# A polynomial-sketch attention and gated feed-forward kernel on one Trainium2 core: batch 1's values loaded ahead of batch 2's queries, other planned durations, and a new set of due times

## The chip, the cores and the metric

The kernel runs on one core of one Trainium2 chip. The metric is the device time of one execution in microseconds. Three runs of the kernel before gave 99.48, 100.64 and 100.89 us, a median of 100.64. A fourth execution, the one that was profiled, took 99.95 us, of which 98.2 lie between the first and the last instruction (the span); every duration below comes from that one.

The engines are called PE (TensorE), DVE (VectorE), ACT (ScalarE), POOL (GpSimd) and SP (SyncE, which here issues nearly all DMAs).

## What is computed

Attention with a product of two small sketches in place of a softmax, then a gated feed-forward block, in these steps (batch 4, heads 4, sequence 1088, head size 32, sketch size 8):

```python
def phi(x):                       # 32 numbers -> 8 x 8 products
    a = einsum('rd,bhsd->bhsr', S1, x); b = einsum('rd,bhsd->bhsr', S2, x)
    return (a outer b).reshape(..., 64)
q_p, k_p = phi(q), phi(k)
kv  = einsum('bhsf,bhsd->bhfd', k_p, v);  z = k_p.sum(axis=2)
x   = einsum('bhsf,bhfd->bhsd', q_p, kv) / (einsum('bhsf,bhf->bhs', q_p, z) + 1e-06)
x   = x.transpose(0, 2, 1, 3).reshape(4352, 128)
out = (maximum(x @ w_gate, 0) * (x @ w_val)) @ w_out      # 128 -> 1536 -> 128
```

## The kernel before

**Tiling.** The feed-forward half is cut into 103 units, numbered 0 to 102. A unit is one bank of the accumulator memory: up to 512 columns of tokens times feed-forward blocks. Unit u is made of these instructions: `g u` (PE, gate product, line 966), `relu u` (ACT, line 971), `v u` (PE, value product, line 978), `h u` (DVE, gate times value, line 988) and `o u` (PE, output product, line 1000). In every sixth unit from 4 on the product goes over POOL: `vcp u` (ACT, line 983) copies the value out of the accumulator, and `hp u` (POOL, line 993) multiplies. A group's last unit ends with `oe u` (ACT, line 1008) and the store `st u` (SP, lines 1017 to 1020). The first six units hold the first 256 tokens; they use the weights third by third, so units 4 and 5 need the last third.

**What stands before it, batch by batch.** For batch b: `kt1 b` (DVE, transposes the keys, line 532), `ksk b` (PE, both sketches of the keys, line 543), `kt2 b` (DVE, transposes them back, line 556), `z b` and `w b` (PE, lines 571 and 585, the sum for the denominator) with the small DVE steps `zc b` and `wc b`, `kphi b` (the outer product, line 600, on POOL; for batch 0 the last two of five pieces are on DVE, by way of an extra transpose into the accumulator, `kt2b`, line 564), `vc b` (casts v to 16 bits, line 607), `kv b` (PE, line 614) and `kve b` (DVE, line 621). On the query side: `qt1 b` (DVE, line 1040), `qsk` (PE, line 736), `qt2` (DVE, line 742), `bw`, `dn`, `rd` and `an` (lines 770, 777, 782 and 802, the denominator and the division), `qphi` (the outer product, line 868, on POOL after the first set). Then a transpose: for the first three groups on PE (`qtr`, line 886) and ACT (`qpt`, line 893), for the other seven a transposing DMA (`qtd`, line 876, issued by SP). `num` (PE, line 902) and `x` (line 909 or 914) give the tokens that the gate and value products read. Batch 0 is split: its first 256 tokens are one set (`0,0`), the rest another (`0,2`).

**Weights.** They arrive as 32-bit thirds (gate `wg0` to `wg2`, value `wv0` to `wv2`, output `wo0` to `wo2`) and are parked in buffers that later hold keys, queries and values: `wst`, lines 251 to 253. A cast (lines 427 and 429, on ACT or POOL by the table `CAST`, line 420) makes 16-bit weights of each and frees its buffer. So a late load waits for a cast: batch 1's v for the cast of the third that was parked in it, batch 2's keys for two others (lines 445 to 451). Batch 2's queries (`q2`) wait for no cast.

**What sets the order.** A planner (class `Plan`, lines 36 to 144) places every step on its engine by the durations that the code gives, by when buffers and accumulator banks come free, and by a due time. Due times follow from the unit numbers (lines 926 and 386 to 387; `D1` is added from unit 6 on) and from a table of hand-made offsets, `shift` (line 1113). Loads are in the plan as instants (`LAND`, line 406) or durations (line 443). The plan's order on each engine is what is built; while the kernel runs, only semaphores decide, and each engine works through its own queue in order. Until the first unit, PE is kept at work by filler matmuls on zeros (line 331).

Of the kernel before, what the change touches and what calls it, by code (L numbers as in the profile page):

```python
# [147 lines left out]
def kernel(  # L148
# [12 lines left out]
    nc = tc.nc  # L161

    B, H, S, D = q.shape
# [46 lines left out]
    def load_k(eng, b):  # L210
        eng.dma_start(out=k_sb[b][:, 0:NC * D], in_=flat(k, b))
# [34 lines left out]
    def half(t, i):  # L246
        return t[:, i * W3:(i + 1) * W3]
# [2 lines left out]
    v1, v2 = (v32[b].rearrange("p h c -> p (h c)") for b in (1, 2))  # L250
    wst = [[half(k_sb[3], 0), half(q_sb[3], 0), half(v2, 0)],
           [half(k_sb[3], 1), half(q_sb[3], 1), half(v2, 1)],
           [half(k_sb[2], 0), half(k_sb[2], 1), half(v1, 0)]]

    def load_w(i):
        c = slice(i * W3, (i + 1) * W3)
# [16 lines left out]
    def load_q(eng, b):  # L273
        eng.dma_start(out=q_sb[b], in_=flat(q, b))

    def load_vs(b):
        for a in (0, 2, 1, 3):
            load_v(nc.sync, b, a)
# [105 lines left out]
    P.banks[S_BANK] = 6.0  # L384
    l_sx = Lease()
    T0, U, SLACK = 11.0, 0.65, 0.25
    D1 = 0.2

    TURN = ["ACT"] * 3 + ["DMA"] * 7

# [12 lines left out]
    def pool(cols):  # L403
        return cols * 0.00188 + 0.07

    LAND = {"k0a": 3.6, "S": 4.3, "k0b": 4.25, "q0a": 5.4, "q0b": 7.3, "v0": 9.75, "wg0": 10.1,
            "wv0": 10.74, "wg1": 11.38, "wv1": 12.02, "wo0": 12.66, "wg2": 13.3, "wv2": 14.94,
            "wo1": 15.58, "k1": 16.94, "wo2": 17.58, "q1": 18.94}
    land = {n: P.landed(n, t) for n, t in LAND.items()}
    P.free["DMA"] = LAND["q1"]  # L410

    def bank(l, i=0):
# [5 lines left out]
    wb_op = P.add("DVE", "WB", 0.15, make_WB, [land["S"]], rec=0.07)  # L418

    CAST = {"wg0": "ACT", "wv0": "POOL", "wg1": "ACT", "wv1": "ACT", "wo0": "POOL",  # L420
            "wg2": "ACT", "wv2": "POOL", "wo1": "POOL", "wo2": "POOL"}
    wcast = {}

    def cast(w, i, eng):
# [12 lines left out]
    issue = {}  # L437

    def load(name, fn, after):
        n = 4 if name[0] == "v" else 1  # L440
        issue[name] = i = P.add("SP", f"{name} issue", 0.44 * n, fn, after,
                                rec=1.95 - 0.44 * n)
        land[name] = P.add("DMA", name, 2.7 if n == 4 else 1.4, None, [i], rec=0.15)

    load("v1", lambda: load_vs(1), [wcast["wo2"]])
    load("k2", lambda: load_k(nc.sync, 2), [wcast["wo0"], wcast["wo1"], issue["v1"]])
    load("q2", lambda: load_q(nc.sync, 2), [])
    load("v2", lambda: load_vs(2), [wcast["wg2"], wcast["wv2"], land["v1"]])
    load("k3", lambda: load_k(nc.sync, 3), [wcast["wg0"], wcast["wv0"]])
    load("q3", lambda: load_q(nc.sync, 3), [wcast["wg1"], wcast["wv1"]])  # L450
# [2 lines left out]
    class K:  # L453


        def __init__(self, b, prev):
# [11 lines left out]
                        rec=0.07)  # L468
# [21 lines left out]
            self.wc_op = P.add("DVE", f"wc {b}", 0.11, self.wc, [w], drop=[lw], rec=0.07)  # L490
            phis = []
            cut = [(0, 2), (2, 4), (4, 6), (6, KX)] if b else [(0, 2), (2, 4), (4, 6), (6, 8), (8, KX)]
            own = [3, 4] if b == 0 else []
            lb = Lease()
            self.lb = lb
            for n, (lo, hi) in enumerate(cut):
# [11 lines left out]
                else:  # L508
                    phis.append(P.add("POOL", f"kphi {b} {lo}", pool(cols),
                                      lambda lo=lo, hi=hi: self.phi(nc.gpsimd, lo, hi), dep))  # L510
            vc = [P.add(e, f"vc {b} {h}", 0.66 if e == "POOL" else 0.58,
                        lambda h=h, e=e: self.vc(h, e), [land[f"v{b}"]],
                        rec=0.0 if e == "POOL" else 0.13)
                  for h, e in enumerate(["ACT", "ACT" if b else "POOL"])]
            lm = Lease()
            self.lm = lm
            self.kvs = []
# [84 lines left out]
                in0=src[:, 0, :, :, None].to_broadcast([128, n, R, R]),  # L602
                in1=bs[:, :, None, :].to_broadcast([128, n, R, R]), op=ALU.mult)

        def vc(self, h, e):
            o, i = (t[self.b][:, 2 * h:2 * h + 2] for t in (v16, v32))
            nc.scalar.copy(out=o, in_=i) if e == "ACT" else nc.gpsimd.tensor_copy(out=o, in_=i)  # L607

        def kv(self, lo, hi, pp):
            m = bank(self.lm)  # L610
# [196 lines left out]
    class G:  # L807


        def __init__(self, qs, b, ks, x0, n, i, col, old, how):  # L810
            self.qs, self.x0, self.n, self.col = qs, x0, n, col
            self.ks, self.b = ks, b
            i = i % NQ
            self.qp, self.pt = q_qp[i], q_pt[i]
            name = f"{self.b},{qs.x0 + x0}"
            phis = []
            if qs.first:
                for x in range(n):
                    phis.append(P.add("DVE", f"qphi {name} {x}", 0.31,
                                      lambda x=x: self.phi(nc.vector, x, x + 1), [qs.o4],  # L820
                                      drop=[qs.la], rec=0.07))
                qs.la.left -= n
            else:
                phis.append(P.add("POOL", f"qphi {name}", pool(n * 256) - 0.02 * n,
                                  lambda: self.phi(nc.gpsimd, 0, n), [qs.o4] + old))
            if how == "DMA":
                pt = P.add("SP", f"qtd {name}", 1.28, self.xpose, phis + old, rec=0.7)
                self.turn = pt
                pt = P.add("DMA", f"qtd {name}", 0.6, None, [pt], rec=0.5)
            else:  # L830
                lt = Lease()
                self.lt = lt
                trs = []
                for x in range(n) if qs.first else [None]:
                    lo, hi = (x, x + 1) if x is not None else (0, n)
                    trs.append(P.add("PE", f"qtr {name} {lo}", pe16(2 * (hi - lo), 128),
                                     lambda lo=lo, hi=hi: self.tr(lo, hi),
                                     [phis[lo] if qs.first else phis[0]], take=[lt]))
                pt = P.add(how, f"qpt {name}",
                           n * 256 / 1920.0 + 0.085 if how == "DVE" else act(n * 256),  # L840
                           lambda: self.tre(how), trs + old, drop=[lt],
                           rec=0.07 if how == "DVE" else 0.13)
            self.pt_op = pt
            ln = Lease()
            self.ln = ln
            num = P.add("PE", f"num {name}", pe16(2, n * 128) if b is not None else
                        pe16(8, 64), self.num,
                        [pt] + [kk.kve for kk in self.ks], take=[ln])
            if qs.first:
                self.x_op = P.add("DVE", f"x {name}", dve(n * 128), self.x_div, [num, qs.rdc],  # L850
                                  drop=[ln], rec=0.07)
            else:
                self.x_op = P.add("ACT", f"x {name}", act(n * 128), self.x, [num], drop=[ln],
                                  rec=0.13)
            self.last = [num, pt] + phis
            qs.last += phis
# [185 lines left out]
    qt1 = {}  # L1042
# [64 lines left out]
    for o in P.ops:  # L1107
# [3 lines left out]


    shift = {
# [24 lines left out]
    }  # L1138
    for o in P.ops:
        o.due += shift.get(o.name, 0.0)  # L1140
# [46 lines left out]
```

## Time and profile before

| what | value |
|---|---|
| median of three runs (lowest, highest) | 100.64 us (99.48, 100.89) |
| the profiled execution: time, span | 99.95 us, 98.2 us |
| granted TensorE clock, mean | 0.995 |
| first gate product (`g 2`) begins | 14.08 us |
| last output products end, last eviction begins | 95.07, 95.09 us |
| idle time of the PE array from 14 us to the end of its work | 0.4 us |
| busy from 25 to 40 us, out of 15: PE, DVE, ACT, POOL | 15.00, 14.80, 14.20, 13.78 us |
| batch 1's v: four issues by SP from 19.05 us | land 2.7 to 3.0 us after the issue |
| batch 2's queries: issued at 12.52 us | land 7.6 us after the issue |

A line of the timeline reads: start, length, engine, source line, operation, output and inputs with their shapes, how many in a row, and in square brackets the idle time before it and what ended it. In the view by windows each engine's entry is its busy time in that stretch and, in brackets, its instructions.

### The profile page before, as it was taken

Reading aid. Unit: us, or ns where it says so; the run is one execution under the profiler, and the core shown is the slowest. Engines: PE = TensorE matmul, PEld = TensorE weight load, DVE = VectorE, ACT = ScalarE, POOL = GpSimd, SP = SyncE. Lnnn points to the kernel's source line nnn. Section 1 sums busy time; section 2 is a strip of 40 time slices with the busy share of each in tenths; the row PEclk is TensorE's granted clock in tenths of the full one; section 3 lists DMA queues with packets and bytes.
Section 4 is the critical chain, followed back from the end, with each engine's and each line's share of the span. In section 5 each row is a group of like instructions: output and inputs, shape, how many; then the busy total and the mean of one; then the engine's idle time right before and its main releaser. Section 6 shows DMA issues by size and latency. Waiting matters only on the chain.

```text
span 98.2 us, 3002 instructions
## 1 busy us (share of the span) xinstructions
PE 93.0 (95%) x1130; PEld 62.1 (63%) x1130; DVE 83.3 (85%) x181; ACT 81.4 (83%) x160; POOL 61.1 (62%) x66
## 2 busy tenths in 40 slices
PE   5979999999999999999999999999999999999960
PEld 2247667866685665665646765777577756768850
DVE  5969987989999999999999899948869676789850
ACT  3402799987999988999998759999999999999930
POOL 6129639789979799699859924999540404314000
PEclk9999999999999999999999999999999999999998
DMA  2999999559830668960436002104480220030031
GB/s 50 308 278 263 405 411 414 218 136 273 259 111 0 147 131 282 321 176 5 108 83 140 0 7 77 30 23 94 107 157 10 53 60 0 0 80 27 0 107 53
DMA packets 16782, 13.26 MB, mean 135 GB/s; under 512 B 8064, under 2 KB 14464, under 8 KB 16768
## 3 DMA queue, kind: packets, MB, share of 16 engines
q1 hardware_dynamic: 16592, 12.95, 45.1%
q8 instruction: 8, 0.13, 0.6%
q10 hardware_dynamic: 176, 0.13, 0.4%
q14 instruction: 6, 0.05, 0.2%
HBM read 9.14 MB, written 2.23 MB: 116 GB/s over the span
## 4 chain that ended last, share of the span: by engine, by line
PE 87%; DMA 5%; DVE 3%; SPq 1%; issue 0%; ACT 0%; DVEq 0%
PE ps L1000 24%; PE ps L966 23%; PE ps L978 22%; DMA q_sb<-in_q_dram 5%; PE ps L902 4%; PE ps L736 3%; PE ps L331 2%; PE ps L614 2%; PE ps L543 2%; PE ps L886 1%; PE ps L571 1%; DVE kab L556 1%; PE ps L585 1%; DVE ht L988 1%; DVE kp L600 1%; PE ps L755 1%
## 5 line engine op out<-in xcount | busy, mean ns | idle before, releaser
L988 DVE TENSOR_TENSOR ht<-g_sb,ps 128x512 f16<-128x512 f16 (+1 forms) x87 | 55.2, 672 | 8.3 <-PE ps L978 4.3
L971 ACT ACTIVATE g_sb<-ps 128x512 f16<-128x512 f32 (+1 forms) x103 | 56.6, 607 | 4.0 <-PE ps L966 2.7
L966 PE MATMUL ps<-xT,wg 128*128 128x512 f16 (+1 forms) x120 | 35.7, 349 | 0.0
L978 PE MATMUL ps<-xT,wv 128*128 128x512 f16 (+1 forms) x120 | 34.8, 347 | 0.0
L1000 PEld LDWEIGHTS <-ht 128*128 128x128 f16 x408 | 25.9, 98 | 9.3 <-DVE ht L988 2.4
L1000 PE MATMUL ps<-wo,ht 128*128 128x128 f16 x408 | 30.7, 219 | 0.4 <-DVE ht L988 0.4
L993 POOL TENSOR_TENSOR ht<-g_sb,v_sb 128x512 f16<-128x512 f16 x16 | 18.7, 1167 | 17.0 <-ACT v_sb L983 9.2
L600 POOL TENSOR_TENSOR kp<-kab 128x512 f16<-128x512 f32 (+1 forms) x15 | 17.0, 1162 | 2.5 <-DVE kab L556 2.3
L966 PEld LDWEIGHTS <-wg 128*128 128x128 f16 x120 | 12.8, 115 | 6.5 <-issue 1.8
L978 PEld LDWEIGHTS <-wv 128*128 128x128 f16 x120 | 13.0, 114 | 5.1
L868 POOL TENSOR_TENSOR qqp<-qan,qabc 128x1024 f16<-128x1024 f32 (+1 forms) x9 | 15.7, 1755 | 0.7 <-DVE qan L802 0.6
L983 ACT COPY v_sb<-ps 128x512 f32<-128x512 f32 x16 | 9.7, 608 | 0.3 <-PE ps L978 0.2
L331 PE MATMUL ps<-zero 128*128 128x512 f16 (+5 forms) x24 | 7.1, 430 | 1.0 <-DVE maskkv L296 1.0
L1040 DVE STREAM_TRANSPOSE qT<-q_sb 128x576 f32<-128x576 f32 (+4 forms) x10 | 6.0, 611 | 0.9 <-DMA q_sb<-in_q_dram 0.9
L1008 ACT ACTIVATE o_sb<-ps 128x512 f32<-128x512 f32 (+1 forms) x10 | 5.4, 539 | 1.6 <-PE ps L1000 1.5
L607 ACT CAST v<-v 128x576 f16<-128x576 f32 x7 | 4.6, 684 | 1.5 <-DMA v<-in_v_dram 1.5
L532 DVE STREAM_TRANSPOSE kT<-k_sb 128x544 f32<-128x544 f32 (+2 forms) x8 | 5.5, 720 | 0.0
L742 DVE STREAM_TRANSPOSE qabc<-ps 128x512 f32<-128x512 f32 (+2 forms) x8 | 5.4, 698 | 0.1
L902 PE MATMUL ps<-qpt,bz 128*128 128x512 f16 (+2 forms) x26 | 5.3, 306 | 0.0
L914 ACT CAST xT<-ps 128x512 f16<-128x512 f32 (+1 forms) x9 | 5.0, 561 | 0.3 <-PE ps L902 0.3
L331 PEld LDWEIGHTS <-zero 128*128 128x128 f16 x24 | 2.4, 116 | 3.3 <-issue 1.4
L770 POOL TENSOR_TENSOR bw<-qabc 128x256 f32<-128x256 f32 (+1 forms) x3 | 2.3, 773 | 2.8 <-DVE qabc L742 2.8
(85 smaller groups left out, 64.0 us busy)
## 6 DMA issues: line engine op xcount, KB each, us to landing
v<-in_v_dram SPq DMA_DIRECT2D x15, 144.0 KB, 5.6
out_dram<-o_sb SPq DMA_DIRECT2D x28, 64.0 KB, 1.8
k_sb<-in_k_dram SPq DMA_DIRECT2D x3, 544.0 KB, 4.0
q_sb<-in_q_dram SPq DMA_DIRECT2D x3, 544.0 KB, 7.3
k_sb<-in_moe_w_out_dram SPq DMA_DIRECT2D x2, 256.0 KB, 5.0
q_sb<-in_q_dram SPq DMA_DIRECT2D x1, 416.0 KB, 5.7
k_sb<-in_k_dram SPq DMA_DIRECT2D x1, 288.0 KB, 2.9
k_sb<-in_k_dram SPq DMA_DIRECT2D x1, 256.0 KB, 3.0
```

The lines of the kernel that those rows point to most:

```text
L331: nc.tensor.matmul(PS[:, W_BANK, 0:m * w], zero, zero[:, None, 0:w].to_broadcast([128, m, w]), start=True, stop=True)
L600: eng.tensor_tensor(out=self.kp[:, lo:hi].rearrange("p x g (i a c) -> p (x g i) a c", i=2, a=R), in0=src[:, 0, :, :, None].to_broadcast([1 ...
L868: eng.tensor_tensor(out=self.qp[:, lo:hi].rearrange("p x g (i a c) -> p (x g i) a c", i=2, a=R), in0=a_in[:, :, :, None].to_broadcast([128 ...
L902: nc.tensor.matmul(o[:, 0:n * 128].rearrange("f (x t) -> f x t", x=n)[:, :, t], self.ks[b or 0].bz[:, p], self.pt[:, 0:n, p, t], start=(p ...
L966: nc.tensor.matmul(bank(self.lg)[:, y * W:(y + 1) * W], wblock(wg, j), x, start=True, stop=True, skip_group_check=True)
L971: nc.scalar.activation(out=self.gs[:, 0:self.cols], in_=bank(self.lg)[:, 0:self.cols], func=ACTF.Relu)
L978: nc.tensor.matmul(bank(self.lv)[:, y * W:(y + 1) * W], wblock(wv, j), x, start=True, stop=True, skip_group_check=True)
L983: nc.scalar.copy(out=self.vs, in_=bank(self.lv))
L988: nc.vector.tensor_tensor(out=self.ht[:, 0:w], in0=self.gs[:, 0:w], in1=bank(self.lv)[:, 0:w], op=ALU.mult)
L993: nc.gpsimd.tensor_tensor(out=self.ht, in0=self.gs, in1=self.vs, op=ALU.mult)
L1000: nc.tensor.matmul(o[:, s], self.ht[:, y * W + s * 128:y * W + (s + 1) * 128], wo[:, j // 4, (j % 4) * DM:(j % 4 + 1) * DM], start=(j == 0 ...
L1040: nc.vector.transpose(qT[b][:, lo * 32:hi * 32], q_sb[b][:, lo * 32:hi * 32])
```

## The change

It moves which third is parked where, gives some steps to other engines, alters numbers in the plan and replaces the table of offsets. Counted in instructions, DVE loses three (the extra transpose and two outer products of batch 0's keys), POOL gains two outer products and the cast of `wg2` and loses the cast of half of batch 0's v, and ACT gains that cast and loses `wg2`'s. All other work is the same and stands in another order.

```diff
-           [half(k_sb[2], 0), half(k_sb[2], 1), half(v1, 0)]]
+           [half(k_sb[2], 0), half(v1, 0), half(k_sb[2], 1)]]
...
-    D1 = 0.2
+    D1 = 0.7
...
-    LAND = {"k0a": 3.6, "S": 4.3, "k0b": 4.25, "q0a": 5.4, "q0b": 7.3, "v0": 9.75, "wg0": 10.1,
-            "wv0": 10.74, "wg1": 11.38, "wv1": 12.02, "wo0": 12.66, "wg2": 13.3, "wv2": 14.94,
-            "wo1": 15.58, "k1": 16.94, "wo2": 17.58, "q1": 18.94}
+    LAND = {"k0a": 3.6, "S": 4.3, "k0b": 4.25, "q0a": 5.4, "q0b": 7.5, "v0": 10.0, "wg0": 10.35,
+            "wv0": 10.99, "wg1": 11.63, "wv1": 12.27, "wo0": 12.91, "wg2": 13.55, "wv2": 15.09,
+            "wo1": 15.73, "k1": 17.09, "wo2": 17.73, "q1": 19.09}
...
-            "wg2": "ACT", "wv2": "POOL", "wo1": "POOL", "wo2": "POOL"}
+            "wg2": "POOL", "wv2": "POOL", "wo1": "POOL", "wo2": "POOL"}
...
-        land[name] = P.add("DMA", name, 2.7 if n == 4 else 1.4, None, [i], rec=0.15)
-
-    load("v1", lambda: load_vs(1), [wcast["wo2"]])
-    load("k2", lambda: load_k(nc.sync, 2), [wcast["wo0"], wcast["wo1"], issue["v1"]])
-    load("q2", lambda: load_q(nc.sync, 2), [])
+        land[name] = P.add("DMA", name, {"k2": 3.6}.get(name, 2.7 if n == 4 else 1.4), None, [i], rec=0.15)
+
+    load("v1", lambda: load_vs(1), [wcast["wo1"]])
+    load("q2", lambda: load_q(nc.sync, 2), [issue["v1"]])
+    load("k2", lambda: load_k(nc.sync, 2), [wcast["wo0"], wcast["wo2"], issue["q2"]])
...
-            own = [3, 4] if b == 0 else []
+            own = [] if b == 0 else []
...
-                  for h, e in enumerate(["ACT", "ACT" if b else "POOL"])]
+            vc = [P.add("ACT", f"vc {b} {h}", 0.58, lambda h=h: self.vc(h), [land[f"v{b}"]],
+                        rec=0.13) for h in range(2)]
...
-                pt = P.add("DMA", f"qtd {name}", 0.6, None, [pt], rec=0.5)
+                pt = P.add("DMA", f"qtd {name}", 2.4 if b == 3 else 0.6, None, [pt], rec=0.5)
...
-        "g 10": -0.4, "g 12": -2.5, "g 16": 0.9, "g 18": 0.4, "g 19": 1.3, "g 2": -3.4,
+        "an 0,2": -3.3, "bw 0,0": -0.9, "bw 2,0": -0.9, "dn 0,0": -3.2, "g 11": -3.1,
...
```

The order that follows, where the prediction speaks of it (everything built, in the order of each engine's queue):

| queue | before | after |
|---|---|---|
| PE, first units | `num 0,0, g 2, v 0, g 0, v 2, g 1, v 1, qtr 0,2, g 3, g 4, g 5, v 3, o 0, num 0,2, o 1, qtr 0,4, v 4` | `num 0,0, g 0, v 0, g 1, qtr 0,2, v 1, g 2, g 4, v 2, g 3, num 0,2, g 5, v 3, o 0, o 1, qtr 0,4, o 2, g 8, v 4` |
| PE, before the keys | `ksk 0, sx, qaT, z 0` | `ksk 0, qaT, sx, z 0` |
| DVE, set 0,2 | `qt2, qt2, qt1, bw, kve 0, dn, rd, x 0,0, an` | `qt2, qt2, qt1, bw, dn, rd, an, kve 0, x 0,0` |
| ACT, first stage | `vc 0, rdx, wg0, qpt, rdTe, wg1, wv1, wg2, relu` | `rdx, vc 0, vc 0, qpt, rdTe, wg0, wv1, wg1, relu` |
| ACT, batch 1's v | `oe 5, relu 12, relu 10, relu 9, vcp 10, vc 1, relu 11, relu 13, vc 1` | `oe 5, relu 7, vc 1, vc 1, relu 9, vcp 10` |
| POOL | `kphi 0` x3, `vc 0, wv0, wo0, qphi 0,2, qphi 0,4, wv2, wo1, wo2, hp 4` | `kphi 0` x5, `wv0, qphi 0,2, wo0, wg2, qphi 0,4, wo1, wv2, wo2, hp 4` |
| SP | `q2, v1, k2, st 5` | `v1, q2, k2, st 5` |
| SP, batch 3 | `qtd 3,0, st 59, qtd 3,4` | `qtd 3,0, qtd 3,4, st 59` |

More of the change, by code (lines that the diff above doesn't have):

```diff
@@ L510, in __init__ @@
                                       lambda lo=lo, hi=hi: self.phi(nc.gpsimd, lo, hi), dep))
-            vc = [P.add(e, f"vc {b} {h}", 0.66 if e == "POOL" else 0.58,
-                        lambda h=h, e=e: self.vc(h, e), [land[f"v{b}"]],
-                        rec=0.0 if e == "POOL" else 0.13)
-                  for h, e in enumerate(["ACT", "ACT" if b else "POOL"])]
+            vc = [P.add("ACT", f"vc {b} {h}", 0.58, lambda h=h: self.vc(h), [land[f"v{b}"]],
+                        rec=0.13) for h in range(2)]
             lm = Lease()
@@ L603, in phi, with vc @@
                 in1=bs[:, :, None, :].to_broadcast([128, n, R, R]), op=ALU.mult)
-        def vc(self, h, e):
-            o, i = (t[self.b][:, 2 * h:2 * h + 2] for t in (v16, v32))
-            nc.scalar.copy(out=o, in_=i) if e == "ACT" else nc.gpsimd.tensor_copy(out=o, in_=i)
+        def vc(self, h):
+            nc.scalar.copy(out=v16[self.b][:, 2 * h:2 * h + 2], in_=v32[self.b][:, 2 * h:2 * h + 2])
         def kv(self, lo, hi, pp):
```

51 rows, old and new, of the table shift are left out of this document.

## The prediction

> **What bounds the kernel now.** I read the page first: engine totals, the chain that ended last, the granted clock.
>
> ```profile
> PE 93.0 (95%) x1130; PEld 62.1 (63%) x1130; DVE 83.3 (85%) x181; ACT 81.4 (83%) x160; POOL 61.1 (62%) x66
> ...
> PEclk9999999999999999999999999999999999999998
> ...
> PE 87%; DMA 5%; DVE 3%; SPq 1%; issue 0%; ACT 0%; DVEq 0%
> ```
>
> 87% of the chain is PE, at full clock. Whether PE is at its pace is seen in the chain in order of time (start, length, line, how many) and in PE's waits from 14 us to the end:
>
> ```profile
> 40.47 1.08 PE ps L978 x5
> ...
> 43.32 0.89 PE ps L1000 x16
> ```
>
> ```profile
> PE ps L1000 <- DVE ht L988: 0.4, 1, 0.4
> ```
>
> Five 512-column matmuls take 1.08 us, 0.217 each; four 128-column ones take 0.223. A unit costs PE 0.217 + 0.217 + 0.223 = 0.66 us. In 81 us the array waited once, 0.4 us, near the end (last `h` to last `o`). So from the first gate product PE is the bound, and a step made earlier anywhere else, after 14 us, is worth nothing unless PE waits for it. What a change can win is the time before the first unit, plus the 0.4. What it can lose is open-ended: each new PE wait is added in full. Last I looked at how much the others have left, 25 to 40 us (busy time of PE, PEld, DVE, ACT, POOL):
>
> ```profile
> 25.00:40.00 15.00, 15.00 (x202) 9.68 (x201) 14.80 (x28) 14.20 (x28) 13.78 (x12) 1.00 0.58 162
> ```
>
> DVE idles 0.2 us in 15. That is the thin cover.
>
> **The first stage.** Here the order changes most. The rows of DVE and POOL before:
>
> ```profile
> 12.50 0.34 DVE L770 TENSOR_TENSOR bw<-qabc 128x192 f32<-128x192 f32 x1
> 12.76 0.28 DVE L621 TENSOR_TENSOR bz<-ps,maskkv 128x128 f16<-128x128 f32 x1
> 12.96 0.37 DVE L777 TENSOR_REDUCE qdn<-bw 128x24 f32<-128x216 f32 x1
> 13.37 0.30 DVE L782 RECIPROCAL qrd<-qdn 128x24 f32<-128x24 f32 x1
> 13.60 0.42 DVE L909 TENSOR_TENSOR xT<-ps,rdT 128x256 f16<-128x256 f32 x1
> 13.95 0.35 DVE L802 TENSOR_TENSOR qan<-qabc,qrd 128x192 f32<-128x192 f32 x1
> ```
>
> ```profile
> 11.32 0.62 POOL L429 CAST wv<-k_sb 128x512 f16<-128x512 f32 x1 [0.27 <-DMA k_sb<-in_moe_w_val_dram]
> 13.18 0.61 POOL L429 CAST wo<-k_sb 128x512 f16<-128x512 f32 x1 [1.25 <-DMA k_sb<-in_moe_w_out_dram]
> 14.37 2.98 POOL L868 TENSOR_TENSOR qqp<-qan,qabc 128x512 f16<-128x512 f32 x2 [0.58 <-DVE qan L802]
> 17.30 0.61 POOL L429 CAST wv<-v 128x512 f16<-128x512 f32 x1
> ...
> 19.78 1.17 POOL L993 TENSOR_TENSOR ht<-g_sb,v_sb 128x512 f16<-128x512 f16 x1 [0.76 <-ACT v_sb L983]
> ```
>
> In the before column, `v 4` begins at 17.96, right after the cast of `wv2` (17.30 + 0.61). So POOL's queue, not the first gate product at 14.08, sets when the units run freely.
>
> *DVE, after.* It loses the extra transpose (0.36) and two outer products (0.69, 0.41). `z 0` now stands behind `qaT` and `sx`, so its end moves from 7.90 to about 8.17. From there in steps of before's starts: `zc` 8.18, two transposes of the queries to 9.23, `bw 0,0` 9.29, its five followers 1.25 to 10.54, two `qt2` 0.97, the small transpose 0.13: `bw 0,2` at 11.64 instead of 12.50. Then `dn` 12.01, `rd` 12.41, `an` 12.76 to 13.10. But `kve 0` now stands behind `an`: it starts at 13.03 instead of 12.76, though its matmuls end by 12.4 (POOL's fifth outer product ends near 11.7, `vc 0`'s second half near 11.9). From `kve` to the first gate product the step was 14.08 - 12.76 = 1.32: the first unit starts at 14.35, 0.27 later.
>
> *POOL, after.* Five `kphi 0`: four steps of 1.03 from 7.00 reach 11.11; the fifth is 128x256, and 768 columns take 1.52, 512 take 1.07, so 0.6: 11.7. `wv0` to 12.25; wait for `an`, 13.13; `qphi 0,2` to 14.16; `wo0`, `wg2` (0.56 each) to 15.28; `qphi 0,4` 1.90 to 17.18; `wo1` 17.73; `wv2` ends 18.35, 0.44 later than before. Between first unit and `v 4`, PE has two more products than before in front of it (`o 2`, `g 8`), 0.22 + 0.22 = 0.44 us of work that no longer follows. Run from 14.35, PE reaches `v 4` at about 18.3 and waits to 18.4. `g 4` comes at 15.7, after `wg2` at 15.3. **First stage: 0.0 us.** The 0.27 is lost in time that PE would have waited anyway; 1.5 us more on POOL is hidden in its old gaps (1.25, 0.58, 0.27) and in the earlier `an`. ACT gains one cast of 0.67, loses one of 0.62: nothing, covered by `rdT`, which is ready at 12.7.
>
> **Unit 4.** On ACT `qpt 0,4` (1.09) and `vcp 4` (0.69) now stand behind `x 0,2` and `relu 5`: `x 0,2` ends near 18.1, `relu 5` starts 17.9, `qpt` 18.4, `vcp` ends 20.0, `hp 4` (1.17) 21.2. PE reaches `o 4` at 20.9. **+0.3 us**; bounds 0 (if ACT is as early as before, 19.70) and 0.5.
>
> **Loads.** `v1` waits for the cast of `wo1` (17.8) instead of `wo2` (19.03): issued 1.2 us earlier. Four issues took 2.5 us and landed 2.7 to 3.0 after issue, with one 544 KB load finishing 1.1 us after the first issue; after, the load of `q1` stands in the same relation (18.83). So v lands near 22.6. `q2` no longer goes at 12.52 but behind v, at 20.3, and `k2` behind that, after the cast of `wo2` (18.9), at 20.8 instead of 21.62; `st 5` behind them needs its eviction at 22.6, so SP holds nothing up. Needed: `kv 1` stands at 27.3 in both orders by the sum of PE's work (0.217, 0.223, and the rows of the small products), `ksk 2` at 30.7 (before 32.2), queries of batch 2 later still. Between ends of 3 us (v1) and 7.6 (q2, then in a crowd) all land by 28. **0.0 us**, and nothing gained, because nothing waited for v1. The longer durations for `k2` and `qtd 3,0` move work away from transfers that were not late: `qtd 3,0` is issued at 64.8 and lands 2.7 later; `num 3,0` runs at 70.8.
>
> **The long middle.** The same PE steps in another order: from `v 4` to the end the sum of rows is 76.1 us before, 75.6 after (18.4 to 94.0; the two products again). What matters is whether DVE keeps up. The tightest run after is `v 8` to `o 21`: 13 products at 0.605, two `qt2` 0.65, two `kt1` 0.67, `qt1` 0.69 and 0.62, `kt2` 0.71, `kve` 0.21, `dn` 0.47, `rd` 0.30 = 13.50 us, 0.25 for the first `v` to get out, against 13.82 of PE work: 0.07 us to spare. The same sum over before has its least at `o 18`, 0.14, and no wait is seen there. **0.0 us**; bounds -0.1 and +0.5, some 0.01 on each of 22 steps and a second such run (`o 38`, 0.30 to spare).
>
> **The end.** After the last full group's `o`, five products remain on DVE in both orders, so the 0.4 us stays; bounds -0.4 and 0.
>
> **Sum:** 0 + 0.3 + 0 + 0 + 0 = +0.3 us on the profiled execution's 99.95 (span 98.2 + 1.75 around it) = 100.25. That execution lies 0.69 below the median of three; all four together average 100.24, which I take as base for another median: **100.5 us**, no change that can be told, as a measurement of this kernel resolves about 2% (98.6 to 102.7).
>
> **A rule that speaks against it.** The only DVE operations with two inputs in SBUF before the units are `bw 0,2` and `an 0,2`, and before, both ran while POOL was idle (11.94 to 13.18, 13.80 to 14.37), so no row shows them beside POOL. After, `bw 0,2` at 11.64 meets POOL's cast of `wv0` (11.7 to 12.3). If one holds the other for its length, `bw` starts up to 0.6 late, and `an`, `qphi`, `wv2` and the first unit with it. The Trainium skill, SBUF — State Buffer, "Who interferes with whom", says a VectorE instruction with two SBUF inputs and a GpSimd one that reads SBUF exclude each other, whoever starts first; by that rule 0.6 us is added, 101.1.
>
> **Rivals.**
> - *Slower: ACT stands still at batch 1's v.* Before, ACT came to `vc 1` at 25.09, 1.3 us after v had landed (23.8). After, it stands behind `relu 7`, near 23.0, against a landing at 22.6: 0.4 to spare. All of ACT queues behind it: `relu 9`, `vcp 10`, and so DVE's `h 9`, on the run with 0.07 to spare. Against: the 3.0 us of this very load. For: the page's median for v is 5.6, and batch 3's took 5.9 to 6.7 behind two 544 KB loads. With 5.6 from the last issue at 20.0 v lands at 25.6, ACT is held 2.6 us; work that PE has in hand hides some 0.5 (an estimate: two products whose banks are free, 0.44): +2.1, 102.6. It decides, beyond 2%, from a landing at about 25.7 on.
> - *The two engines exclude each other*, the 0.6 above, all of it on the path through `an` and `wv2`: 100.5 + 0.6 = 101.1.
> - *Faster: POOL's chain ends earlier.* If DVE's relief comes through with `an` at 12.7, POOL's wait (12.25 to 13.13) shrinks by 0.4, `wv2` and `v 4` come 0.4 earlier, the wait at `o 4` is gone, and the last wait may go (0.4): 100.24 - 0.4 - 0.4 = 99.4. Against: `an` needs nine DVE steps whose lengths are known. PE's pace leaves no more than this.
>
> **How the numbers follow.** No change as summed, 0.56: the sum rests on rows, and PE's own work is the same to 0.1 us. Exclusion, 0.12: no row for or against it. ACT held, 0.20: one row against, an average for it; 0.04 of this is shorter holds that stay within 2%, 0.16 goes beyond. Faster, 0.12: two things have to come at once; 0.04 of it I give to more than 2%, as single runs of before spread by 1.4 us. So faster by over 2% 0.04, within 2% 0.56 + 0.12 + 0.04 + 0.08 = 0.80, slower by over 2% 0.16. The range that leaves 0.2 out runs from just under the faster case to the held one: 99.3 to 102.6. The likeliest case alone, by its bounds (0 and 0.5 at unit 4, -0.1 and +0.5 in the middle, -0.4 at the end): 99.7 to 101.2.
>
> **What would show it.** First gate product at 14.3 and `v 4` at 18.4, just behind the cast of `wv2`; POOL's wait before `qphi 0,2` shrunk; `hp 4` ending near 21.2 with PE's weight load waiting for it; ACT not idle before `vc 1`; PE without waits of over 0.3 us from 22 to 92. Wrong: an idle ACT before line 604 (the v cast), several PE waits on `ht` between 25 and 50, or a first unit at 13.7 or before.

## The result and the profile after

| | before | after |
|---|---|---|
| median (runs; lowest, highest) | 99.86 us (22; 98.95, 101.64) | 100.58 us (22; 99.88, 101.67) |
| the profiled execution: time, span | 99.95, 98.2 us | 100.27, 98.5 us |
| ratio, 95% interval | | 1.0070 [1.0048, 1.0093] |

The medians hold every run; the ratios leave out runs over 1.5% above the fastest of the same kernel.

The change costs 0.7 us. The number forecast, 100.5, lies 0.1 below the time measured, but that is luck: two errors of opposite sign made it fit. The kernel before takes 99.86 and not the 100.24 that was put under the sum, and the loss is 0.5 to 0.7 us and not 0.3. So "no change" was wrong: there is a small loss.

The page after. PE's total is 93.4 us for 93.0, and the chain that ended last has 80% of PE for 87%, because it now runs back through a transfer in the first stage:

```profile
PE 93.4 (95%) x1131; PEld 62.8 (64%) x1131; DVE 82.7 (84%) x178; ACT 81.1 (82%) x160; POOL 62.7 (64%) x68
...
PE 80%; DMA 12%; SPq 2%; DVE 1%; issue 1%; POOL 1%; ACT 0%; DVEq 0%
```

PE's waits from 13 us on (us in total, times, longest), and the stretch from 25 to 40 us (busy time of PE, PEld, DVE, ACT, POOL):

```profile
PE ps L963 <- POOL wg L429: 0.6, 1, 0.6
```

```profile
25.00:40.00 15.00, 14.97 (x200) 9.69 (x199) 14.68 (x28) 13.77 (x27) 14.29 (x12) 1.00 0.58 157
```

Before's wait of 0.4 at the end is gone from this list, and a new one of 0.6 stands in the first stage: `g 4` waits for the cast of `wg2`. The rows of DVE and POOL that answer to those shown of before:

```profile
10.68 0.34 DVE L767 TENSOR_TENSOR bw<-qabc 128x192 f32<-128x192 f32 x1
...
11.81 0.36 DVE L799 TENSOR_TENSOR qan<-qabc,qrd 128x192 f32<-128x192 f32 x1
12.09 0.28 DVE L618 TENSOR_TENSOR bz<-ps,maskkv 128x128 f16<-128x128 f32 x1
```

```profile
12.25 1.07 POOL L865 TENSOR_TENSOR qqp<-qan,qabc 128x512 f16<-128x512 f32 x1 [0.67 <-DVE qan L799]
...
14.78 0.62 POOL L429 CAST wg<-v 128x512 f16<-128x512 f32 x1 [0.91 <-DMA v<-in_moe_w_gate_dram]
15.36 1.95 POOL L865 TENSOR_TENSOR qqp<-qan,qabc 128x1024 f16<-128x1024 f32 x1
17.26 0.61 POOL L429 CAST wo<-v 128x512 f16<-128x512 f32 x1
17.81 0.62 POOL L429 CAST wv<-v 128x512 f16<-128x512 f32 x1
```

`bw 0,2` comes at 10.68 (forecast 11.64), `an` at 11.81 (12.76). But POOL gets nothing out of it: it stands idle for 0.91 us in front of `wg2`, which lands late, and ends `wv2` at 18.43, where 18.35 was forecast. On PE:

```profile
13.40 0.38 PE L963 MATMUL ps<-xT,wg 128*128 128x256 f16 x2
...
15.45 0.41 PE L963 MATMUL ps<-xT,wg 128*128 128x256 f16 x2 [0.57 <-POOL wg L429]
...
18.48 0.84 PE L975 MATMUL ps<-xT,wv 128*128 128x256 f16 x6
...
19.48 0.71 PE L541 MATMUL ps<-kT,wS 64*32 64x288 f32 x16
...
21.06 0.39 PE L997 MATMUL ps<-wo,ht 128*128 128x128 f16 x4
21.55 0.35 PE L569 MATMUL ps<-kab 128*32 128x32 f32 x18
...
25.05 0.38 PE L975 MATMUL ps<-xT,wv 128*128 128x256 f16 x2
```

The row at 19.48 is `ksk 1`. Up to it both orders have run the same number of products, so its start can be compared directly; before it was at

```profile
19.41 0.71 PE L543 MATMUL ps<-kT,wS 64*32 64x288 f32 x16
...
93.51 1.54 PE L1000 MATMUL ps<-wo,ht 128*128 128x128 f16 x24 [0.36 <-DVE ht L988]
```

Before takes 93.51 + 1.54 - 19.41 = 75.64 us from `ksk 1` to the last output product; after, the last row is

```profile
93.25 2.09 PE L997 MATMUL ps<-wo,ht 128*128 128x128 f16 x24
```

and the stretch 93.25 + 2.09 - 19.48 = 75.86 us. So in this pair 0.07 us are lost ahead of `ksk 1` and 0.22 behind it. The wait at the end has not gone: the same 24 products now wait in small pieces inside 2.09 us. The list of waits hides this, as it hides some 0.2 us each at `z 1` (0.49 from `o 4` at 21.06 to 21.55, where before takes 0.31) and at `v 9` (25.05; eight matmuls of 0.055 from 24.41 end by 24.85).

### The profile page after: what moved, and what is told of

The parts are those of the page before. It is cut to its first block, busy times and chain, and to the rows that moved or that the text cites. A ratio compares the mean times of both kernels' runs of the same rounds, so it can differ in the third digit from the quotient of the medians.

```text
span 98.5 us, 2985 instructions
## 1 busy us (share of the span) xinstructions
PE 93.4 (95%) x1131; PEld 62.8 (64%) x1131; DVE 82.7 (84%) x178; ACT 81.1 (82%) x160; POOL 62.7 (64%) x68
## 4 chain that ended last, share of the span: by engine, by line
PE 80%; DMA 12%; SPq 2%; DVE 1%; issue 1%; POOL 1%; ACT 0%; DVEq 0%
PE ps L997 23%; PE ps L975 22%; PE ps L963 22%; DMA v<-in_moe_w_gate_dram 6%; DMA v<-in_v_dram 5%; PE ps L899 4%; PE ps L733 2%; PE ps L541 2%; PE ps L611 2%; DVE ht L985 1%; PE ps L569 1%; POOL wg L429 1%; PE ps L883 1%; PE ps L583 1%; SPq L235 0%
## 5 line engine op out<-in xcount | busy, mean ns | idle before, releaser
L968 ACT ACTIVATE g_sb<-ps 128x512 f16<-128x512 f32 (+1 forms) x103 | 55.7, 612 | 4.2 <-PE ps L963 3.3
L963 PE MATMUL ps<-xT,wg 128*128 128x512 f16 (+1 forms) x120 | 34.9, 348 | 0.6 <-POOL wg L429 0.6
L975 PE MATMUL ps<-xT,wv 128*128 128x512 f16 (+1 forms) x120 | 33.8, 348 | 0.0
L997 PE MATMUL ps<-wo,ht 128*128 128x128 f16 x408 | 31.7, 219 | 0.1
L997 PEld LDWEIGHTS <-ht 128*128 128x128 f16 x408 | 26.7, 98 | 7.9 <-DVE ht L985 1.1
L598 POOL TENSOR_TENSOR kp<-kab 128x512 f16<-128x512 f32 (+2 forms) x17 | 18.6, 1125 | 1.3 <-DVE kab L554 1.3
L331 PE MATMUL ps<-zero 128*128 128x512 f16 (+4 forms) x25 | 7.1, 404 | 1.0 <-DVE maskkv L296 1.0
L1037 DVE STREAM_TRANSPOSE qT<-q_sb 128x512 f32<-128x512 f32 (+4 forms) x10 | 6.0, 604 | 0.0
L604 ACT CAST v<-v 128x576 f16<-128x576 f32 x8 | 5.2, 676 | 0.4 <-DMA v<-in_v_dram 0.3
L611 PEld LDWEIGHTS <-kp 128*128 128x128 f16 (+1 forms) x72 | 3.2, 98 | 1.5 <-issue 0.3
```

The costliest lines, as they stand in the source:

```text
L331: nc.tensor.matmul(PS[:, W_BANK, 0:m * w], zero, zero[:, None, 0:w].to_broadcast([128, m, w]), start=True, stop=True)
L598: eng.tensor_tensor(out=self.kp[:, lo:hi].rearrange("p x g (i a c) -> p (x g i) a c", i=2, a=R), in0=src[:, 0, :, :, None].to_broadcast([1 ...
L963: nc.tensor.matmul(bank(self.lg)[:, y * W:(y + 1) * W], wblock(wg, j), x, start=True, stop=True, skip_group_check=True)
L968: nc.scalar.activation(out=self.gs[:, 0:self.cols], in_=bank(self.lg)[:, 0:self.cols], func=ACTF.Relu)
L975: nc.tensor.matmul(bank(self.lv)[:, y * W:(y + 1) * W], wblock(wv, j), x, start=True, stop=True, skip_group_check=True)
L997: nc.tensor.matmul(o[:, s], self.ht[:, y * W + s * 128:y * W + (s + 1) * 128], wo[:, j // 4, (j % 4) * DM:(j % 4 + 1) * DM], start=(j == 0 ...
```

## The experiments

Each kernel is compared with the kernel before on the same chip. Times in us; `v 4`, `ksk 1` and the stretch from `ksk 1` to the end of the last output product are from the one profiled execution of each, the medians from many. A profiled execution need not be a usual one: that of e3 is the fastest of its twelve, 99.88 against a median of 100.50.

| kernel | median (runs) | ratio to before | `v 4` | `ksk 1` | `ksk 1` to last `o` |
|---|---|---|---|---|---|
| before; once more (b1) | 99.86 (22); 100.52 (1) | | 17.96; 17.85 | 19.41; 19.29 | 75.64; 75.64 |
| after | 100.58 (22) | 1.0070 [1.0048, 1.0093] | 18.48 | 19.48 | 75.86 |
| after, once more (a2) | 100.38 (12) | 1.0046 [1.0012, 1.0080] | 18.46 | 19.46 | 76.12 |
| e1 | 100.60 (12) | 1.0061 [1.0028, 1.0094] | 18.53 | 19.50 | 75.73 |
| e2 | 100.74 (12) | 1.0067 [1.0029, 1.0106] | 18.31 | 19.31 | 76.56 |
| e3 | 100.50 (12) | 1.0091 [1.0058, 1.0124] | 18.13 | 19.11 | 75.84 |
| e4 | 100.51 (12) | 1.0065 [1.0026, 1.0103] | 17.59 | 18.59 | 76.19 |
| e5 | 101.15 (6) | 1.0130 [1.0063, 1.0196] | 18.35 | 19.35 | 76.63 |
| e6 | 101.64 (6) | 1.0168 [1.0111, 1.0226] | 19.10 | 20.08 | 76.69 |
| g1 | 100.64 (12) | 1.0078 [1.0045, 1.0111] | 18.11 | 19.19 | 76.22 |
| g2 | 100.44 (12) | 1.0060 [1.0024, 1.0096] | 18.20 | 19.20 | 76.38 |
| g3 | 100.54 (12) | 1.0054 [1.0018, 1.0090] | 17.91 | 18.99 | 76.31 |
| g4 | 101.79 (6) | 1.0184 [1.0128, 1.0240] | 18.51 | 20.22 | 77.30 |
| before, delayed (d1) | 102.72 (6) | 1.0289 [1.0232, 1.0346] | 20.30 | 21.75 | 75.63 |
| after, delayed (d2) | 103.12 (6) | 1.0337 [1.0266, 1.0407] | 20.77 | 21.77 | 76.06 |

### The last gate third and the order of the loads (e1 to e4)

First theory A: the loss is the wait at `g 4` and POOL's queue behind the cast of `wg2`. Rivals: B, it is spread over the order behind unit 4; C, it is the loads' new order. The edits, in the order of each queue:

```diff
e1 -POOL wo0, wg2, qphi 0,4        -ACT relu 1, qpt 0,2
   +POOL wo0, qphi 0,4             +ACT relu 1, wg2, qpt 0,2
e2 -PE v 1, g 2, g 4, v 2, g 3, num 0,2, g 5, v 3, o 0
   +PE v 1, g 2, v 2, g 3, num 0,2, v 3, g 4, g 5, o 0
e3  both
e4 -SP v1, q2, k2
   +SP q2, v1, k2
```

> The changed kernel with one edit: the cast of the last gate third is given back to ACT, where it stands behind relu 1 (as for ACT, so for POOL all other orders stay). Theory A (the loss lies at the last gate third: PE waits 0.57 us for its cast at g 4, and POOL's qphi 0,4, wo1 and wv2 queue behind the same cast): PE's wait at g 4 stays, as the third lands at 14.7 whoever casts it, but POOL's qphi 0,4 starts near 13.9 instead of 15.36 and wv2 ends near 17.2 instead of 18.4, so v 4 comes 0.3 to 0.4 us earlier: about 100.2 against 100.6. Theory B (the first stage costs nothing, the loss is in the order after unit 4): within 0.1 of the changed kernel. Theory C (the loss comes from the loads' new order): within 0.1.

> The changed kernel with one edit: on PE, g 4 and g 5 stand behind v 3, so that products which need no late weights fill PE's 0.57 us wait. The cast of the third stays on POOL. Theory A in its POOL form (the queue behind the cast is what counts): v 4 still waits for wv2 at 18.4, so 0 to -0.1 us, about 100.5. If PE's wait at g 4 is itself the loss: -0.5, about 100.0. Theory B: within 0.1 of 100.6. Theory C: within 0.1.

> Both edits: the cast of the last gate third on ACT, and g 4 and g 5 behind v 3. Theory A: neither PE's wait nor POOL's queue is left, v 4 near 17.5 to 17.7 instead of 18.48, so -0.7 to -0.9 us: about 99.8, as fast as the kernel before or a little faster. More than the sum of the two alone if each hides the other. Theory B: less than 0.2 gained. Theory C: within 0.1.

> The changed kernel with one edit: batch 2's queries are issued ahead of batch 1's v again, without a wait, as before. Theory C (the loads' new order is what costs): -0.5 to -0.7 us, about 100.0. Theories A and B: nothing waits for either load, so within 0.15 of 100.6, with v landing up to 1 us later behind the 544 KB of queries and ACT idle before its cast by up to that.

All four take 100.50 to 100.74, as the changed kernel does. The wait moves where the cast goes: in e1 PE waits 0.6 for ACT's cast of `wg2`, in e3 0.6 at `num 0,2`, whose `qpt` stands on ACT behind that cast. In e2 the wait at `g 4` is gone and another has come. PE's wait, and ACT's rows at batch 1's v, of e2:

```profile
PE ps L975 <- ACT g_sb L968: 0.7, 1, 0.7
```

```profile
23.79 1.25 ACT L604 CAST v<-v 128x576 f16<-128x576 f32 x2 [0.80 <-DMA q_sb<-in_q_dram]
24.95 0.59 ACT L968 ACTIVATE g_sb<-ps 128x512 f16<-128x512 f32 x1
```

ACT reaches the cast 0.80 before v has landed (the row names the transfer of `q2`, which runs beside v's; the cast reads v alone, all four quarters of it). `relu 9` stands behind both casts, and `v 9` needs the bank that it frees. That is the prediction's slower rival on a small scale. C falls: with before's order of issues (e4) the time is the same. A is not enough either: e4's profile has no wait at `g 4` and reaches `ksk 1` at 18.59, 0.89 earlier than after, but ends only 0.56 earlier (94.78 against 95.34), because the casts hold PE again (0.3 at 24.48).

### Batch 1's v later on ACT (e5, e6), and both kernels once more (b1, a1)

D: ACT stands at batch 1's v. E: the profiled execution of before is a late starter, so that a pair of profiles understates the loss.

```diff
e5 -ACT oe 5, relu 7, vc 1, vc 1, relu 9, vcp 10, relu 10, relu 13
   +ACT oe 5, relu 7, relu 9, vcp 10, relu 10, vc 1, vc 1, relu 13
e6  as e5, and
   -POOL wo0, wg2, qphi 0,4                       +POOL wo0, qphi 0,4
   -ACT qpt 0,2, relu 2, relu 3, relu 4, x 0,2    +ACT qpt 0,2, wg2, relu 2, relu 3, x 0,2, relu 4
   -PE g 2, g 4, v 2, g 3, num 0,2, g 5, v 3, o 0, o 1
   +PE g 2, v 2, g 3, num 0,2, v 3, o 0, o 1, g 4, g 5
b1, a1  before and after, unchanged
```

> The changed kernel with one edit: on ACT the two casts of batch 1's v stand behind relu 10 instead of behind relu 7. Theory D (the rival of the prediction: ACT stands at the head of its queue for batch 1's v, and PE then waits for a bank near 25 us; 0.2 us of PE wait in the profile of the changed kernel, 0.9 in that of the edit with g 4 behind v 3, where v landed 0.5 us later): the PE wait at 25 us is gone, and the time falls by what ACT waits in a usual execution, -0.3 to -0.6 us, to 100.0 to 100.3. Theory B (the loss is spread over the new order after unit 4): less than 0.15 gained. Theory A has fallen in the runs above as a theory of the whole loss; it expects nothing here.

> The changed kernel with the waits of its first 26 us taken away together: the last gate third cast on ACT behind the eviction of the second query group, g 4 and g 5 behind o 1, relu 4 behind the second token eviction, and batch 1's v cast late as in the run beside it. Theories A and D together: no PE wait from 13.4 to 18, v 4 at 17.6 to 17.9 instead of 18.48, none at 25: -0.8 to -1.2 us against the changed kernel, 99.4 to 99.8, at or below the kernel before. Theory B: less than 0.3 gained, since the loss would lie behind.

> The kernel before, unchanged, for a second profile. In the first one the first quarter of the queries landed at 6.26 us, in five profiles of the changed kernel and its variants at 4.5 to 5.4, though the issues are the same. Theory E (the profile of before is a late starter, and before's usual start is earlier than the profile showed, so the prediction was summed on too late a base): queries at about 5.3, first gate product near 13.2, v 4 near 17.1 to 17.4 instead of 17.96, span 97.4 to 97.7. If before always starts as in its first profile: span 98.1 to 98.3, first gate product near 14.1.

> The changed kernel, unchanged, for a second profile beside the second one of before. Theory D: ACT waits before the cast of batch 1's v and PE waits near 25 us, together 0.2 to 0.9 us. Theory A: PE waits at g 4 again unless the last gate third lands before 14.0. If neither wait is there and the span is still above before's by 0.5 or more, the loss is in what stands behind 26 us (theory B).

e5 is slower than the change. Its rows of ACT, then of PE:

```profile
25.63 1.26 ACT L604 CAST v<-v 128x576 f16<-128x576 f32 x2
26.76 2.33 ACT L968 ACTIVATE g_sb<-ps 128x512 f16<-128x512 f32 x4
```

```profile
27.43 0.38 PE L963 MATMUL ps<-xT,wg 128*128 128x512 f16 x1 [0.70 <-ACT g_sb L968]
```

The two casts are 1.26 us in which ACT gives PE no bank, wherever they stand together. e6 has the same 0.7 at 28.23 and waits at two output products besides (0.3, 0.2). In b1 the first part of the queries is ready at 5.2 us, a microsecond earlier than in before's first profile, and yet `v 4` comes at 17.85: as E was put, it falls. In a1 the whole first stage came some 4 us late: its trace shows PE at half pace until some 16 us and DVE waiting for it (the last section has the rows). What a1 shows of the change is the stretch behind `ksk 1`, 75.88.

### Mixed orders (f2 to f4), and after once more (a2)

The order of each engine was written down and built anew, so that one kernel's order could be followed up to a point and the other's from there; lines of these kernels stand some 60 further down.

```diff
f2  after's engines and order up to v 4;   then before's order, before's loads
f3  before up to o 31 (some 41 us);        then after's order
f4  after up to o 15 (some 29 us);         then before's order
a2  after, unchanged
```

> The kernel of this run has the changed kernel's engines and its order on PE, DVE, ACT and POOL up to v 4 (the first 18 us), and from there the order of the kernel before, with the loads parked and issued as in the kernel before. Three theories of where the 0.7 us lies. Start (the first 18 us: POOL's longer queue, the late last gate third): ratio to before 1.007, as the change itself. Middle (18 to 30 us: ACT at batch 1's v, kt2 1 at z 1): 1.000, about 99.9 us. Rest (the new order after 30 us): 1.000 as well.

> The kernel before, with its own engines and loads, its own order up to o 31 (some 41 us) and the changed kernel's order from there. Start: 1.000, near 99.9 us. Middle: 1.000. Rest, if it lies behind 41 us: 1.007, near 100.6 us; the trace then has more PE waits behind 41 us than before's one of 0.4.

> The changed kernel, with its engines, loads and order up to o 15 (some 29 us), and from there the order of the kernel before. Start: 1.007. Middle: 1.007, with the wait of PE for ACT's copy near 25 us in the trace. Rest: 1.000. If f2 comes out at 1.000 and this one at 1.007, the loss lies between 18 and 30 us.

> The changed kernel once more, beside the three mixed ones on the same chip: 1.007 by every theory; what it gives is the value that the others are held against.

f2 1.0132 [1.0054, 1.0210], f3 1.0134 [1.0070, 1.0198], f4 1.0285 [1.0218, 1.0353]: every mixture is slower than the kernel before. f4 is also clearly slower than after; the intervals of f2 and f3 overlap with after's. f4 has some 0.9 us of PE stalls from 32 to 34 us, right behind its seam. No run builds a kernel's own order in this way, so what the building costs by itself is not known, and the three tell nothing of the place. a2 tells most. Its rows of PE and ACT:

```profile
14.35 0.38 PE L963 MATMUL ps<-xT,wg 128*128 128x256 f16 x2
...
18.46 0.85 PE L975 MATMUL ps<-xT,wv 128*128 128x256 f16 x6
...
21.28 0.40 PE L997 MATMUL ps<-wo,ht 128*128 128x128 f16 x4
...
25.29 0.38 PE L975 MATMUL ps<-xT,wv 128*128 128x256 f16 x2 [0.21 <-ACT g_sb L968]
```

```profile
22.63 0.59 ACT L968 ACTIVATE g_sb<-ps 128x512 f16<-128x512 f32 x1
23.49 1.25 ACT L604 CAST v<-v 128x576 f16<-128x576 f32 x2 [0.27 <-DMA q_sb<-in_q_dram]
24.65 0.59 ACT L968 ACTIVATE g_sb<-ps 128x512 f16<-128x512 f32 x1
```

Here the first stage comes as forecast within 0.06: first gate product 14.35 (14.35), `v 4` 18.46 (18.4), `o 4` just behind `hp 4`'s end at 21.23 (21.2). And one wait is there that the sum did not have: ACT is idle for v (0.27), `relu 9` comes at 24.65, and `v 9` starts 0.4 behind PE's pace.

### The single waits taken away (g1 to g4)

```diff
g1 -ACT vc 1, vc 1, relu 9, vcp 10       +ACT vc 1, relu 9, vcp 10, vc 1
g2 -DVE h 5, qt1 1, kt2 1, qt1 1         +DVE h 5, kt2 1, qt1 1, qt1 1
   -PE g 6, g 11, o 4, z 1, o 5          +PE g 6, g 11, z 1, o 4, o 5
g3  g1 and g2
g4  g3, and
   -POOL qphi 0,4, wo1, wv2              +POOL qphi 0,4, wv2, wo1
   -PE o 2, g 8, v 4                     +PE v 4, o 2, g 8
   -ACT vc 1, relu 9, vcp 10, vc 1       +ACT relu 9, vcp 10, vc 1, vc 1
```

> On ACT the second cast of batch 1's v stands behind vcp 10 (relu 9 and vcp 10 run between the two casts); all else as changed. In the second profile of the changed kernel relu 9 began at 24.65, behind the casts, though its product had ended at 24.2, and PE waited at v 9 (25.29, 0.4 us over its pace). Theory small waits: 0.2 to 0.4 us gained, ratio to before about 1.003, and no PE excess between 24 and 26 us. Rival moved block: as when both casts stood behind relu 10, the time held moves to 27 us and the ratio stays at 1.006 or more. Rival elsewhere (the loss is in the first stage's spread, not in waits behind v 4): 1.006 and the wait gone.

> On DVE kt2 1 stands ahead of qt1 1's first half and on PE z 1 ahead of o 4; all else as changed. Theory small waits: the 0.2 us at z 1 or o 4 near 21.4 is gone, ratio about 1.004. Rival elsewhere: 1.006, wait gone.

> The two edits above together. Theory small waits: both waits gone, 0.4 to 0.6 us gained, ratio 1.000 to 1.002, about 100.0 us; behind v 4 the trace then takes what before's took. Rival elsewhere: 1.005 or more with no PE wait of over 0.2 us between 19 and 60.

> As the one before, and the first stage's end in before's manner: POOL casts wv2 ahead of wo1, PE runs v 4 ahead of o 2 and g 8, and both casts of batch 1's v stand apart behind vcp 10 (v lands 0.6 us later, since wo1 is cast later). Theory start: v 4 near 17.9 with two products after it, 0.1 us gained on the one before. Theory small waits: the same as the one before within 0.2 us.

These four were built like f2 to f4. The waits go in part, and the time stays. PE's rows of g1:

```profile
24.69 0.38 PE L1038 MATMUL ps<-xT,wv 128*128 128x256 f16 x2
...
28.32 1.03 PE L1026 MATMUL ps<-xT,wg 128*128 128x512 f16 x4
29.35 0.84 PE L1060 MATMUL ps<-wo,ht 128*128 128x128 f16 x12
```

`v 9` runs at 24.69 without its wait, 0.36 earlier than in the first profile of after (0.29 of it is g1's earlier `ksk 1`); at 29.35 (four products of 0.217 from 28.32 end at 29.19) 0.17 of it is gone while an output product waits for DVE's `h`, and the last `o` ends at 95.41, 0.07 later than there. In g3 the wait at `o 4` is gone, `v 9` (24.82) still starts 0.15 behind PE's pace, and a new wait stands at `w 1` (line 646):

```profile
PE ps L646 <- ACT o_sb L1068: 0.3, 1, 0.3
```

g4, which gives up the head start that the change gave batch 1's v, is 1.8% slower than before; in its profile `bw 0,2` is also held for 0.43 us by POOL's cast (last section), so the edit alone may not be the cause. No single wait that was tried carries the loss.

### Late loads taken out of both (d1, d2)

```diff
+    late = sb([128, 512], FP32, "late")
+    nc.vector.memset(late, 0.0)
+    for _ in range(6):
+        nc.vector.tensor_scalar_mul(out=late, in0=late, scalar1=1.0)
-    warm(3584)
+    warm(3584 + 3 * 2280)
```

> The kernel before with seven idle operations on DVE ahead of its first transpose, so that the whole first stage starts some 3 us later and no query, value or weight third lands late for it; the filler on PE is made as much longer. What counts is the difference to the next kernel, the changed one with the same delay. Here: all weight casts start without waiting for a load, time about 102.5 to 103.

> The changed kernel with the same delay. Theory landings (the changed first stage loses because loads come late for it, in some runs more than in others): the difference to the delayed kernel before shrinks to 0.2 us or less. Theory order (POOL's longer queue ahead of v 4, ACT at batch 1's v, DVE without slack behind): it stays at 0.5 to 0.7 us.

103.12 - 102.72 = 0.40 us remain with all loads early; the lowest of each, 102.71 and 102.27, differ by 0.44. That lies between the 0.2 of theory landings and the 0.5 of theory order, and the two ratios' intervals overlap, so the times alone do not choose. The profiles show a part of the loss that stays: the stretch from `ksk 1` to the last `o` takes 75.63 to 75.64 us in all three profiles of before's order, and 75.86, 75.88, 76.06 and 76.12 in the four of after's. So theory order stands for 0.2 to 0.5 us of the loss; whether landings carry the rest is not shown. This pair also shows the place cleanest. PE's rows of d1, then of d2, and one row of d2's DVE:

```profile
20.30 0.41 PE L982 MATMUL ps<-xT,wv 128*128 128x256 f16 x2
...
21.75 0.72 PE L547 MATMUL ps<-kT,wS 64*32 64x288 f32 x16
...
95.84 1.54 PE L1004 MATMUL ps<-wo,ht 128*128 128x128 f16 x24 [0.36 <-DVE ht L992]
```

```profile
20.77 0.85 PE L979 MATMUL ps<-xT,wv 128*128 128x256 f16 x6
...
21.77 0.75 PE L545 MATMUL ps<-kT,wS 64*32 64x288 f32 x16
...
22.91 0.60 PE L967 MATMUL ps<-xT,wg 128*128 128x256 f16 x4
23.59 0.40 PE L1001 MATMUL ps<-wo,ht 128*128 128x128 f16 x4
...
67.77 0.39 PE L1001 MATMUL ps<-wo,ht 128*128 128x128 f16 x4
68.29 0.38 PE L967 MATMUL ps<-xT,wg 128*128 128x512 f16 x1
...
95.73 2.10 PE L1001 MATMUL ps<-wo,ht 128*128 128x128 f16 x24
```

```profile
67.55 2.48 DVE L989 TENSOR_TENSOR ht<-g_sb,ps 128x512 f16<-128x512 f16 x4 [0.66 <-PE ps L979]
```

`ksk 1` differs by 0.02 us, the end by 97.83 - 97.38 = 0.45. All of it lies behind `ksk 1`: at `o 4`, where four products of 0.109 from 22.91 end at 23.35 and PE goes on at 23.59, behind `hp 4` (0.24); near 68, where four matmuls of 0.055 from 67.77 end at 67.99 and the next product waits until 68.29 for a bank that DVE's `h` frees (0.3). DVE had stood idle for 0.66 ahead of that `h`, waiting for a value product, so it was not short of time there. Together 0.5; elsewhere the new order is 0.1 faster.

## Why the prediction was right or wrong

- **The base, and the call of "no change".** This is the step that made the forecast wrong. 100.24 was the mean of four runs, 99.86 is the median of 22, 0.38 lower. It hid the sign: 100.24 + 0.3 lies below the median of 100.64 that was shown, while 99.86 + 0.3 is a loss. The reason given for "no change", that a measurement resolves about 2%, does not hold either: 22 runs each resolved 0.2% here.
- **The first stage, 0.0.** Right in the profiled pairs: `ksk 1` differs by 0.02 (d1, d2) and by 0.07 (the first pair). That a2 follows the working within 0.06 is luck in part: PE ran at half pace until some 7 us there (the two `qaT` products take 0.93 us, 0.70 in the first profile of after), and so came as late as the forecast had it from the late queries in before's profile (landed at 6.26). In the first profile of after the first gate product came at 13.40, one of the prediction's own signs of being wrong, and a late `wg2` ate the gain up. The rival "faster" had its condition (`an` at 11.81) and gave nothing, since POOL then waited for `wg2`.
- **Unit 4, +0.3.** Right: 0.24 at `o 4` in d2 and in a2, with `hp 4` ending at 21.23 in a2. In the first profile `hp 4` ended at 20.84 and `z 1` waited instead for `kt2 1` (0.2).
- **The loads, 0.0.** The step of the mechanism that failed: "v lands near 22.6", with ACT coming at 23.0 and 0.4 to spare. The first issue was at 17.89, as forecast, and the last at 19.2; but v was complete only at 23.2 and 23.5 (first profile, a2), 4.0 and 4.3 us behind the last issue and not 2.6. ACT was there at 23.2 in both. So it had nothing to spare, and stood idle for 0.27 in a2, which is the other sign of being wrong. PE then lost 0.2 and 0.4 at `v 9`; in a1 and d2, where v came in time, it lost nothing there.
- **The long middle, 0.0.** Right about what it summed: no profile of after has PE waiting for DVE's `h` in the tight run from `v 8` to `o 21`, so the 0.07 us to spare was enough. What was lost between unit 4 and the end was lost for other reasons: at `v 9`, and in d2 near 68 us (0.3), where the cause behind the late value product is open.
- **The end, 0.0.** Right: from the last value product's pass to the end of the output products before took 2.06 us (92.99 to 95.05), after 2.09 (93.25 to 95.34).
- **ACT held** came true at nothing to a fifth of its price of 2.1, as v was complete over 2 us before the point from which it decides (25.7).
- **The exclusion** did not come as forecast in after: `bw 0,2` was held for 0.11 in a2 and not for 0.6. More of it is below.

By the means of the profiles, 0.1 us is lost up to `ksk 1` (19.47 against 19.35, leaving out a1 and the delayed pair) and 0.34 behind it (75.98 against 75.64): 0.2 at unit 4, 0 to 0.4 at `v 9`, 0 to 0.3 near 68, less the 0.1 that the new order gains elsewhere. Together that is 0.46, which accounts for a2 (1.0046) but not for all of the 0.72 between the medians: some 0.3 stays open. The first pair of profiled executions differs by only 0.32, as before's lies 0.09 above its median and after's 0.31 below. The open part may lie ahead of `ksk 1`, where executions of one kernel differ most, but no profile shows it. No version was found that beats the kernel before.

## What to carry to other kernels

Where an engine must not come late, ask how far the time of what it waits for may move: 0.4 us of cover (time to spare) on ACT was worked out from one landing, and the landing came 0.6 to 0.9 us later than that. The cover of 0.07 us on DVE, which rests on the engines' own rows, held. Removing the wait that a trace shows is no proof of its worth: the wait at `g 4` (e2) and the one at `v 9` (e5, g1) were removed, each time another came further on, and the time did not fall. And a prediction about a few tenths stands on the base first: with four runs that spread by 1.4 us, say how far the base itself may be off, and do not call a few tenths no change before knowing what many runs resolve.

## What the runs showed of the hardware

**VectorE beside GpSimd.** In some executions `bw 0,2` (two inputs in SBUF) runs beside POOL's cast of `wv0`. DVE's and POOL's rows in a2, then in e5, then in g4:

```profile
11.53 0.45 DVE L767 TENSOR_TENSOR bw<-qabc 128x192 f32<-128x192 f32 x1
```

```profile
11.15 0.61 POOL L429 CAST wv<-k_sb 128x512 f16<-128x512 f32 x1
```

```profile
11.53 0.34 DVE L767 TENSOR_TENSOR bw<-qabc 128x192 f32<-128x192 f32 x1
```

```profile
11.58 0.77 POOL L429 CAST wv<-k_sb 128x512 f16<-128x512 f32 x1
```

```profile
11.78 0.77 DVE L830 TENSOR_TENSOR bw<-qabc 128x192 f32<-128x192 f32 x1
```

```profile
11.73 0.61 POOL L492 CAST wv<-k_sb 128x512 f16<-128x512 f32 x1 [0.68 <-DMA k_sb<-in_moe_w_val_dram]
```

The one that starts first keeps its length (0.61, 0.34, 0.61), and the other is longer: by 0.11 in a2 (0.45 for 0.34, an overlap of 0.23), by 0.16 in e5 (0.77 for 0.61, an overlap of 0.29) and by 0.43 in g4 (0.77 for 0.34, an overlap of 0.56). In all three the later one pays the overlap less 0.12 to 0.13 us. The Trainium skill, SBUF — State Buffer, "Who interferes with whom", has it that the first holds the port for its whole instruction and the other blocks fully. The three pairs agree, but for those 0.12 to 0.13 us. The prediction's 0.6, by that rule, would need `bw 0,2` to start together with the cast; the most that any of these shows is the 0.43 of g4.

**PE's pace at the start.** PE begins every profiled execution at half pace: filler matmuls of 512 columns follow each other every 0.43 us at first, and every 0.22 once it is at full pace. When it changes differs from run to run. The same two products (`qaT`) in the first profile of after and in a1:

```profile
5.82 0.70 PE L744 MATMUL ps<-qT,SA 128*128 128x256 f32 x2
```

```profile
7.21 1.22 PE L744 MATMUL ps<-qT,SA 128*128 128x256 f32 x2
```

In the first PE is at full pace from some 4.7 us on, in a2 from some 7, in a1 from some 16, and a1's first gate product comes at 18.12 where the first profile has 13.40. The profile's granted clock reads 1.00 in all three through these stretches, so it does not tell the two paces apart here. No run sets the moment of the change.

**The same load lands differently from run to run.** `wg2`, issued at 8.42 and 8.81 us in two executions of the same kernel, landed at 14.7 and 13.6. The trace's packets hold a fetch of instructions of about 1 us at 12.60 in the first and at 12.85 in the second. Whether the fetch held the load up is not shown: it stands near the load in both, and no experiment moved it.
